# Where the tiles of a gated attention and MLP kernel lie in the SBUF: one stack of pools, or two

## The chip, the cores and the metric

The kernel runs on one core of a Trainium2 chip. The metric is the device time of one execution in microseconds (us), as the median of several runs; smaller is better. A profile comes from one further execution, which has a time of its own. Addresses are bytes from the start of an SBUF partition, in thousands ("51.3 K" is byte 51,328); every tile takes the same bytes in each partition that it uses.

## The reference

`x` is 2048 x 448, float32. A sigmoid gate mixes two branches, row by row:

```
g   = sigmoid(x . gate_w)
q, k, v = x @ wqkv                      # 16 heads of 28
a   = local attention of each row over 8 rows: itself and every second one before it
a   = a @ wo
b   = square(relu(x @ w1 + b1)) @ w2 + b2      # 448 -> 1792 -> 448
out = g * a + (1 - g) * b
```

## The kernel before

**Arithmetic.** Float32 matrices are split into a high part of type float32r and a low part (the remainder), made by ScalarE (copy to float32r) and VectorE (subtract). A product takes three matmuls: high x high, high x low, low x high. Of a matmul's two operands one is loaded into the array (the stationary one; the profile's PEld rows) and the other is streamed through it (the moving one; the PE rows). In a row such as `h<-x1b,w1h` the moving operand stands first, the stationary one second.

**Phase A (to about 110 us).** The 2048 rows are four chunks of 512 columns of the transposed `x`. For each chunk TensorE computes q, k and v. Line 244 does the first 36 matmuls over all 128 rows; after that line 176 (`side_by_side`) issues matmuls of 64 rows in pairs, one for each half of the array. The moving operand is the weight (`wqh`, `wql`, `w7h`, `w7l`), the stationary one `x`. ScalarE evacuates to staging tiles `st` (line 195), and stores go to DRAM (`q_d`, `k_d`, `v_d`). Loads and splits of `w1` and of half of `w2` lie in the same phase.

**Phase B.** The MLP runs over the chunks in the order 3, 0, 1, 2. A step f (14 in each chunk) is a block `h` of 11 matmuls with 512 columns (line 620; moving `x`, stationary `w1`) and a block `b` of 12 matmuls with 448 columns (line 684, `mlp_o`; moving `w2`, stationary `hh` and `hl`), two steps behind. Between them ScalarE does relu and two squares (lines 626 to 628) and VectorE the low part `hl` (line 629). `w2` has two halves: steps 0 to 6 use `w2ah`, `w2al`, steps 7 to 13 `w2bh`, `w2bl`. Beside it GpSimd multiplies and VectorE reduces for the attention (lines 308, 315, 309, 321). From the third chunk on, finished attention tiles are transposed (lines 702, 703; moving `ident`) and multiplied by `wo` (line 725, blocks `a` of 11 matmuls, moving `woh`, `wol`, `wo7`).

**Order.** The program is written in the order that is run: `advance` counts TensorE time, and callbacks (`at`, `soon`, `later`) put splits, loads and attention pieces between. All DMAs are issued by SyncE, in order. `x` of chunks 0 to 2 is spilled to DRAM and reloaded by `x_reload` (line 609) into a ring of five tiles: `x0` to `x3` of `xpool` and a fifth, `x4`, of `phase_b`.

**Where tiles lie.** Pools are stacked one above the other in the order in which they are opened. The pools `phase_a` and `rawp` are closed at line 584 (`actx.close()`), and `phase_b` takes their place; `reuse_waits="tile"` makes each new tile wait for the users of the tiles that lay at its bytes. In the built program this gives:

| tiles | before, K | role for TensorE |
|---|---|---|
| w1h, w1l, w17 | 1.2 to 51.3 | stationary |
| w2ah, w2al | 51.3 to 76.4 | moving |
| ident | 78.3 | moving |
| x of chunks 1 and 3, ring tiles x0 to x3 (`xpool`) | 79.2 to 95.6 | stationary in phase A, moving in B |
| k, v, q of the attention, softmax, products, o | 95.6 to 145.7 | (o: stationary in the transposes) |
| wqh, wql, w7h, w7l (phase A) | 145.7 to 185.4 | moving |
| x of chunks 0 and 2 (phase A) | 185.4 to 201.8 | stationary |
| st, raw (phase A) | 201.8 to 228.9 | |
| w2bh, w2bl (phase B) | 145.7 to 170.8 | moving |
| woh, wol, wo7 (phase B) | 170.8 to 183.4 | moving |
| w2raw, bt (phase B) | 183.4 to 199.5 | |
| ring tile x4 (phase B) | 199.5 to 203.6 | moving |
| hh, hl (phase B) | 203.6 to 215.9 | stationary |
| od, oh, ol, o7, o8 (phase B) | 215.9 to 225.1 | stationary |

Of the kernel before, what the change touches and what calls it, by code (L numbers as in the profile page):

```python
# [8 lines left out]
F32 = mybir.dt.float32  # L9
F32R = mybir.dt.float32r  # L10
# [4 lines left out]
S, D, H, DH, W, F = 2048, 448, 16, 28, 8, 1792  # L15
P = 128
# [3 lines left out]
G = 4  # L20
HG = H // G
C = HG * DH
NF = F // P
CH = 512
NQ = D + 2
# [21 lines left out]
ST_BUFS = 3  # L47
# [4 lines left out]
def gated_mix_kernel(ctx: ExitStack, tc: tile.TileContext, xT, wqkv, w1, w2, wo, b1, b2, out):  # L52
    nc = tc.nc

    def f32(ap):
        return ap.bitcast(F32)
# [6 lines left out]
    x_d = tc.dram_tile([3, 4, P, 2, CH], F32, name="x_d")  # L63
    f_d = tc.dram_tile([2, NS, P, D], F32, name="f_d")

    const = ctx.enter_context(tc.tile_pool(name="const", bufs=1))
    psum = ctx.enter_context(tc.tile_pool(name="psum", bufs=1, space=bass.MemoryType.PSUM))


# [1 line left out]
    w1l = const.tile([P, 3, F], F32R, name="w1l")  # L71
    w17 = const.tile([P, F], F32R, name="w17")
    NFA = NF // 2
    w2ah = const.tile([P, NFA, D], F32R, name="w2ah")
    w2al = const.tile([P, NFA, D], F32R, name="w2al")
    b1t = const.tile([P, NF], F32, name="b1t")
    b2t = const.tile([P, D], F32, name="b2t")
    ident = const.tile([P, P], F32, name="ident")
    mask = const.tile([P, NS, W], F32, name="mask")
    zt = const.tile([P, 2, NS], F32, name="zt")  # L80
    gt = const.tile([P, 2, NS], F32, name="gt")
    g1t = const.tile([P, 2, NS], F32, name="g1t")

    xpool = ctx.enter_context(tc.tile_pool(name="xpool", bufs=1))
    attp = ctx.enter_context(tc.tile_pool(name="attp", bufs=1))
    smp = ctx.enter_context(tc.tile_pool(name="smp", bufs=2))
    prodp = ctx.enter_context(tc.tile_pool(name="prodp", bufs=1))
    opool = ctx.enter_context(tc.tile_pool(name="opool", bufs=1))

    ctx.enter_context(tc.manual_schedule())  # L90
    make_identity(nc, ident)
# [30 lines left out]
    def x_tiles(c, pool):  # L122
        return X([pool.tile([P, 2, CH], F32R, tag=f"x{j}", name=f"x{c}_{j}") for j in range(4)])
# [19 lines left out]


    actx = ExitStack()
    ap = actx.enter_context(tc.tile_pool(name="phase_a", bufs=1, reuse_waits="tile"))
    rawp = actx.enter_context(tc.tile_pool(name="rawp", bufs=2, reuse_waits="tile"))
    wqh = ap.tile([P, 3, 3, NQ], F32R, name="wqh")
    wql = ap.tile([P, 3, 3, NQ], F32R, name="wql")

    w7h = ap.tile([P, 2, NQ], F32R, name="w7h")
    w7l = ap.tile([P, 2, NQ], F32R, name="w7l")

    halo0 = smp.tile([2 * G * HALO, C], F32, tag="lg", name="halo0")
    nc.gpsimd.memset(halo0, 0.0)
# [1 line left out]
    stage = {}  # L157
# [31 lines left out]
    def qkv_evacuate(pt, c, tl, b):  # L189
        par, t = c // 2, (c % 2) * 4 + tl  # L190
        first = (b, t // 2) not in stage
        if first:
            stage[b, t // 2] = ap.tile([P, G, 2, C], F32, tag="stage", name=f"st{c}_{tl}_{b}", bufs=ST_BUFS)
        st = stage[b, t // 2]
        nc.scalar.activation(st[:, :, t % 2], pt[:, :D].rearrange("p (g c) -> p g c", g=G), AF.Copy)  # L195
        if not first:
            stage.pop((b, t // 2))
            t0 = t - t % 2
            dst, off = ((q_d, 0), (k_d, HALO), (v_d, HALO))[b]
            dd = dst[par, :, off:off + SP].rearrange("g (p s) c -> p g s c", s=NS)[:, :, t0:t0 + 2]  # L200
            nc.sync.dma_start(dd.rearrange("p g s c -> p g (s c)"), st.rearrange("p g s c -> p g (s c)"))
        if b == 0:
            nc.scalar.activation(zt[:, par, t:t + 1], pt[:, D:D + 1], AF.Copy)
# [18 lines left out]
    def run(c, todo, steps):  # L222


        a = 0
        for e, done, *turns in steps:
            side_by_side(todo[0][a:e], todo[1][a:e])
            while a < e:
                advance(min(12, e - a) * MM448)
                a = min(a + 12, e)  # L230
            for one, two in turns:
                turn(one, two)
            for b, tl, acc in done:
                assert acc.todo == 0
                qkv_evacuate(acc.pt, c, tl, b)
# [190 lines left out]
    def at(dt, fn):  # L426

        later.append((clock["pe"] + dt, fn))
# [76 lines left out]
        raws.append(raw)  # L505
    raw7 = attp.tile([P, D], F32, tag="q", name="wqraw7")
    nc.sync.dma_start(raw7, wqkv[2, :, 3, :D])
    x = x_tiles(0, ap)
    for k in range(3):
        nc.scalar.activation(wqh[:, k, 0], raws[0][:, k, :NQ], AF.Copy)  # L510
        parts = (slice(0, 256), slice(256, CH)) if k == 0 else (slice(0, CH),)
# [20 lines left out]
    xs = {0: x}  # L532
# [1 line left out]
    SPLIT_AT = {1: 19000.0, 2: 35000.0, 3: 53500.0}  # L534

    def x_begin(c):
        xs[c] = x_tiles(c, xpool if c % 2 else ap)

    def x_more(c):
        xraw[c] = x_load(c)  # L540
# [13 lines left out]
    for c, t in SPLIT_AT.items():  # L554
        when(t, x_begin, c)
        for k in range(4):
            when(t + k * 900.0, lambda c, k: x_split(xraw[c], xs[c], k), c, k)
        if c < 3:
            when(t + 4500.0, x_more, c + 1)
            when(t + 5000.0, lambda c: x_spill(c, xs[c]), c)  # L560
# [8 lines left out]
    for c in range(4):  # L569
        x = xs[c]  # L570
# [13 lines left out]
    actx.close()  # L584


    bp = ctx.enter_context(tc.tile_pool(name="phase_b", bufs=1, reuse_waits="tile"))
    w2bh = bp.tile([P, NFA, D], F32R, name="w2bh")
    w2bl = bp.tile([P, NFA, D], F32R, name="w2bl")
    woh = bp.tile([P, 3, D], F32R, name="woh")  # L590
    wol = bp.tile([P, 3, D], F32R, name="wol")
    wo7 = bp.tile([P, D], F32R, name="wo7")

    def w2hl(f):
        if f < NFA:
# [8 lines left out]
    def x_reload(i, j):  # L604

        c = ORDER[i]
        r = (4 * i + j) % RING
        xt = (xpool if r < 4 else bp).tile([P, 2, CH], F32R, tag=f"x{r}", name=f"x{c}b_{j}")
        nc.sync.dma_start(f32(xt), x_d[c, j])
        return xt  # L610

# [9 lines left out]
        return pt  # L621

    def mlp_act(pt, c, f):
        hh = bp.tile([P, CH], F32R, tag="hh", name=f"hh{c}_{f}", bufs=3)
        hl = bp.tile([P, CH], F32R, tag="hl", name=f"hl{c}_{f}", bufs=3)
        nc.scalar.activation(pt, pt, AF.Relu, bias=b1t[:, f:f + 1])  # L626
        nc.scalar.activation(hh, pt, AF.Square)  # L627
        nc.scalar.activation(pt, pt, AF.Square)  # L628
        at(HL_DELAY, lambda: nc.vector.tensor_sub(hl, pt, f32(hh)))  # L629
        hs[c, f] = (hh, hl)  # L630
# [142 lines left out]
    for i, c in enumerate(ORDER):  # L773
        if i < 3:
            nxt = [x_reload(i + 1, j) for j in range(early)]
        for f in range(NF):
            pt = mlp_h(x, c, f)
            if f == NF - 4:
                for tl in range(4):
                    fin_fetch(c // 2, (c % 2) * 4 + tl)  # L780
            if f == NF - 1 and i < 3:
                nxt += [x_reload(i + 1, j) for j in range(early, 4)]
            advance(11 * MM512)
            mlp_act(pt, c, f)
            pend.append((c, f))
            lag = 0 if f == NF - 1 and i < 3 else 2
            wo_ready()
            if i > 0:
                wo_step()
            while len(pend) > lag:  # L790
                mlp_o(*pend.pop(0))
                advance(12 * MM448)
        if i < 3:
            x = X(nxt)
# [52 lines left out]
```

## Time and profile before

| | us |
|---|---|
| median of 3 runs (436.4 to 436.87) | 436.61 |
| the profiled execution | 436.64 |
| its span, first to last instruction | 434.9 |
| around the span | 1.7 |
| TensorE busy in the span (2516 matmuls) | 429.1 |
| weight loads busy (2516) | 385.9 |
| GpSimd, VectorE, ScalarE busy | 274.8, 257.9, 179.3 |
| granted TensorE clock, mean | 0.998 |

How to read it: matmuls follow one another through the array, so the duration of one (363 ns for 448 columns) is longer than the distance to the next (about 200 ns); a busy TensorE row is no measure of speed. What counts is how far apart the starts of successive blocks are. The chain of waits in order of time shows that: each piece has its start, its length and the number of matmuls in it.

### The profile page before, as it was taken

The numbers are of one execution on the slowest core, as the hardware profiler recorded it, in microseconds if no ns is written. First come the engines' busy times: TensorE is split into PE (matmuls) and PEld (weight loads), VectorE is DVE, ScalarE is ACT, GpSimd is POOL, SyncE is SP. The second block draws the span as 40 slices with busy tenths as digits, with TensorE's granted clock in tenths as the row PEclk, the third lists the DMA queues.
The fourth block names the chain that finished last, engine by engine and source line by source line (L and its number), as shares of the span: only waits on it lengthen the run. The fifth ranks groups of instructions, "written<-read, shape, count | busy, mean of one in ns | idle before, by whom it ended". The sixth has DMA issues, their size and how long they took to land.

```text
span 434.9 us, 6554 instructions
## 1 busy us (share of the span) xinstructions
PE 429.1 (99%) x2516; PEld 385.9 (89%) x2516; DVE 257.9 (59%) x384; ACT 179.3 (41%) x372; POOL 274.8 (63%) x167
## 2 busy tenths in 40 slices
PE   8999999999999999999999999999999999999996
PEld 7999999999888888888888888888888888888895
DVE  4421322375589977976646776644676856755453
ACT  3542454444554444533433454333523433334530
POOL 1000001940999999999998897945499998785000
PEclk9999999999999999999999999999999999999999
DMA  7989899938723307703203651401427400210013
GB/s 224 365 299 346 223 391 287 356 80 298 260 89 119 142 2 259 254 29 121 78 2 121 223 199 36 151 21 44 142 86 260 172 1 0 76 68 0 2 63 128
DMA packets 33199, 65.44 MB, mean 150 GB/s; under 512 B 2704, under 2 KB 26256, under 8 KB 32784
## 3 DMA queue, kind: packets, MB, share of 16 engines
q1 hardware_dynamic: 33168, 65.02, 43.0%
q8 instruction: 20, 0.33, 0.3%
q14 instruction: 11, 0.09, 0.1%
HBM read 41.23 MB, written 23.77 MB: 149 GB/s over the span
## 4 chain that ended last, share of the span: by engine, by line
PE 97%; DMA 1%; DVE 1%; SPq 0%; issue 0%; ACT 0%
PE h L620 33%; PE b L684 31%; PE qkv L176 22%; PE a L725 8%; PE oT L702 1%; PE qkv L244 1%; DMA xraw<-xT 1%; PE oT L703 0%; SPq L499 0%; SPq L494 0%; DVE bt L660 0%; DVE wql L513 0%; DVE x L514 0%; DVE ol L102 0%; ACT o L101 0%
## 5 line engine op out<-in xcount | busy, mean ns | idle before, releaser
L308 POOL TENSOR_TENSOR qk<-q,k 128x896 f32<-128x896 f32 x64 | 138.6, 2193 | 103.4 <-DMA k<-k_d 72.5
L315 POOL TENSOR_TENSOR av<-lg,v 128x896 f32<-128x896 f32 x64 | 122.3, 2006 | 13.2 <-DVE o L321 7.1
L626 ACT ACTIVATE h<-h,b1t 128x512 f32<-128x512 f32 x56 | 37.0, 662 | 157.6 <-PE h L620 157.6
L176 PE MATMUL qkv<-wqh,x 64*128 64x448 f32 (+1 forms) x528 | 86.8, 363 | 0.0
L629 DVE TENSOR_TENSOR hl<-h,hh 128x512 fp32r<-128x512 f32 x56 | 38.6, 688 | 62.1 <-ACT h L628 61.9
L309 DVE TENSOR_REDUCE lg<-qk 128x32 f32<-128x896 f32 x64 | 66.9, 1076 | 3.9 <-POOL qk L308 3.9
L321 DVE TENSOR_REDUCE o<-av 128x112 f32<-128x896 f32 x64 | 66.6, 1072 | 0.0
L176 PEld LDWEIGHTS qkv<-wqh,x 64*128 64x128 f32 x528 | 59.6, 185 | 0.6
L176 PE MATMUL qkv<-wql,x 64*128 64x448 f32 (+1 forms) x264 | 56.5, 363 | 0.0
L195 ACT ACTIVATE st<-qkv 128x448 f32<-128x448 f32 x48 | 24.7, 544 | 48.4 <-PE qkv L176 39.9
L684 PE MATMUL b<-w2bl,hh 128*128 128x448 f32 x112 | 40.9, 365 | 0.0
L684 PE MATMUL b<-w2bh,hl 128*128 128x448 f32 x112 | 40.9, 365 | 0.0
L684 PE MATMUL b<-w2bh,hh 128*128 128x448 f32 x112 | 40.9, 365 | 0.0
L684 PE MATMUL b<-w2ah,hh 128*128 128x448 f32 x112 | 40.7, 364 | 0.0
L684 PE MATMUL b<-w2ah,hl 128*128 128x448 f32 x112 | 40.6, 362 | 0.0
L684 PE MATMUL b<-w2al,hh 128*128 128x448 f32 x112 | 40.5, 362 | 0.0
L627 ACT ACTIVATE hh<-h 128x512 fp32r<-128x512 f32 x56 | 33.6, 599 | 3.6 <-DMA v_d<-st 1.9
L628 ACT ACTIVATE h<-h 128x512 f32<-128x512 f32 x56 | 33.2, 593 | 0.0
L176 PEld LDWEIGHTS qkv<-wql,x 64*128 64x128 f32 x264 | 30.8, 185 | 0.3
L620 PE MATMUL h<-x1b,w1h 128*128 128x512 f32 x84 | 28.6, 395 | 0.0
L620 PE MATMUL h<-x2b,w1h 128*128 128x512 f32 x84 | 28.5, 393 | 0.0
L620 PE MATMUL h<-x0b,w1h 128*128 128x512 f32 x84 | 28.4, 391 | 0.0
(108 smaller groups left out, 761.0 us busy)
## 6 DMA issues: line engine op xcount, KB each, us to landing
k<-k_d SPq DMA_DIRECT2D x8, 840.0 KB, 5.1
v<-v_d SPq DMA_DIRECT2D x8, 840.0 KB, 4.6
x_d<-x SPq DMA_DIRECT2D x12, 512.0 KB, 5.5
q_d<-st SPq DMA_DIRECT2D x8, 448.0 KB, 8.0
k_d<-st SPq DMA_DIRECT2D x8, 448.0 KB, 5.1
v_d<-st SPq DMA_DIRECT2D x8, 448.0 KB, 6.7
w1raw<-w SPq DMA_DIRECT2D x4, 896.0 KB, 9.9
q<-q_d SPq DMA_DIRECT2D x8, 448.0 KB, 3.4
```

The lines of the kernel that those rows point to most:

```text
L176: nc.tensor.matmul(acc.pt[:, :acc.n], a[rows], w[rows], start=acc.todo == 21, stop=acc.todo == 1)
L308: nc.gpsimd.tensor_mul(pr, q[:, s:s + 1].to_broadcast([P, W, C]), k[:, s:s + W])
L309: pending.append(lambda: nc.vector.tensor_reduce(lg[:, s], pr.rearrange("p w (h d) -> p w h d", h=HG), axis=AX.X, op=ALU.add))
L315: nc.gpsimd.tensor_mul(pr.rearrange("p (h d) w -> p w h d", h=HG), lg[:, s][:, :, :, None].to_broadcast([P, W, HG, DH]), v[:, s:s + W].rea ...
L321: pending.append(lambda: nc.vector.tensor_reduce(o[:, g * C:(g + 1) * C], pr, axis=AX.X, op=ALU.add))
L620: nc.tensor.matmul(pt, w, a, start=i == 0, stop=i == len(pr) - 1)
L626: nc.scalar.activation(pt, pt, AF.Relu, bias=b1t[:, f:f + 1])
L627: nc.scalar.activation(hh, pt, AF.Square)
L628: nc.scalar.activation(pt, pt, AF.Square)
L629: at(HL_DELAY, lambda: nc.vector.tensor_sub(hl, pt, f32(hh)))
L684: nc.tensor.matmul(bps[tl][:, :D], a[:, sl], w, start=f == 0 and i == 0, stop=f == NF - 1 and i == 2)
L725: nc.tensor.matmul(pa[:, :D], a, w, start=i == 0, stop=i == len(pr) - 1)
```

## The change

All pools get a side: `side="left"` pools stack up from the lower end, `side="right"` pools from the upper end. Tiles that TensorE streams go to left pools (`low`, `xpool`, `wqp`, then `phase_b_low`), everything else to right pools. `phase_a` is cut into `wqp` (left), `xap` and `stp` (right), and `hh`, `hl` get a pool of their own, `hidden`. No shape, buffer count or instruction is changed.

| tiles | after, K |
|---|---|
| w2ah, w2al | 1.2 to 26.2 |
| ident | 26.2 |
| x of chunks 1 and 3, ring tiles x0 to x3 | 26.8 to 43.1 |
| wqh, wql, w7h, w7l (phase A) | 43.1 to 82.8 |
| w2bh, w2bl; woh, wol, wo7; ring tile x4 (phase B) | 43.1 to 68.2; 68.2 to 80.8; 80.8 to 84.9 |
| st; raw; x of chunks 0 and 2 (phase A) | 83.2 to 94.0; 94.0 to 110.4; 110.4 to 126.8 |
| w2raw, bt; od to o8; hh, hl (phase B) | 89.1 to 105.2; 105.2 to 114.5; 114.5 to 126.8 |
| o, products, softmax, k, v, q | 126.8 to 176.9 |
| w1h, w1l, w17 | 176.9 to 227.0 |

```diff
-    const = ctx.enter_context(tc.tile_pool(name="const", bufs=1))
+    low = ctx.enter_context(tc.tile_pool(name="low", bufs=1, side="left"))
+    const = ctx.enter_context(tc.tile_pool(name="const", bufs=1, side="right"))
...
-    w2ah = const.tile([P, NFA, D], F32R, name="w2ah")
-    w2al = const.tile([P, NFA, D], F32R, name="w2al")
+    w2ah = low.tile([P, NFA, D], F32R, name="w2ah")
+    w2al = low.tile([P, NFA, D], F32R, name="w2al")
...
-    ident = const.tile([P, P], F32, name="ident")
+    ident = low.tile([P, P], F32, name="ident")
...
-    xpool = ctx.enter_context(tc.tile_pool(name="xpool", bufs=1))
-    attp = ctx.enter_context(tc.tile_pool(name="attp", bufs=1))
+    xpool = ctx.enter_context(tc.tile_pool(name="xpool", bufs=1, side="left"))
+    attp = ctx.enter_context(tc.tile_pool(name="attp", bufs=1, side="right"))
...
-    ap = actx.enter_context(tc.tile_pool(name="phase_a", bufs=1, reuse_waits="tile"))
-    rawp = actx.enter_context(tc.tile_pool(name="rawp", bufs=2, reuse_waits="tile"))
-    wqh = ap.tile([P, 3, 3, NQ], F32R, name="wqh")
+    wqp = actx.enter_context(tc.tile_pool(name="wqp", bufs=1, side="left", reuse_waits="tile"))
+    xap = actx.enter_context(tc.tile_pool(name="xap", bufs=1, side="right", reuse_waits="tile"))
+    rawp = actx.enter_context(tc.tile_pool(name="rawp", bufs=2, side="right", reuse_waits="tile"))
+    stp = actx.enter_context(tc.tile_pool(name="stp", bufs=ST_BUFS, side="right", reuse_waits="tile"))
+    wqh = wqp.tile([P, 3, 3, NQ], F32R, name="wqh")
...
-    bp = ctx.enter_context(tc.tile_pool(name="phase_b", bufs=1, reuse_waits="tile"))
-    w2bh = bp.tile([P, NFA, D], F32R, name="w2bh")
-    woh = bp.tile([P, 3, D], F32R, name="woh")
+    bl = ctx.enter_context(tc.tile_pool(name="phase_b_low", bufs=1, side="left", reuse_waits="tile"))
+    hp = ctx.enter_context(tc.tile_pool(name="hidden", bufs=3, side="right", reuse_waits="tile"))
+    bp = ctx.enter_context(tc.tile_pool(name="phase_b", bufs=1, side="right", reuse_waits="tile"))
+    w2bh = bl.tile([P, NFA, D], F32R, name="w2bh")
+    woh = bl.tile([P, 3, D], F32R, name="woh")
...
-        xt = (xpool if r < 4 else bp).tile([P, 2, CH], F32R, tag=f"x{r}", name=f"x{c}b_{j}")
+        xt = (xpool if r < 4 else bl).tile([P, 2, CH], F32R, tag=f"x{r}", name=f"x{c}b_{j}")
...
-        hh = bp.tile([P, CH], F32R, tag="hh", name=f"hh{c}_{f}", bufs=3)
-        hl = bp.tile([P, CH], F32R, tag="hl", name=f"hl{c}_{f}", bufs=3)
+        hh = hp.tile([P, CH], F32R, tag="hh", name=f"hh{c}_{f}")
+        hl = hp.tile([P, CH], F32R, tag="hl", name=f"hl{c}_{f}")
```

## The prediction

> **What bounds the kernel now.** I read the page first, then who waited for whom on TensorE, then the chain of waits in order of time.
>
> ```profile
> PE 429.1 (99%) x2516; PEld 385.9 (89%) x2516; DVE 257.9 (59%) x384; ACT 179.3 (41%) x372; POOL 274.8 (63%) x167
> ...
> PE 97%; DMA 1%; DVE 1%; SPq 0%; issue 0%; ACT 0%
> ```
>
> TensorE is busy all along, and 97% of the chain that ends last is TensorE. Its list of waits has a single entry:
>
> ```profile
> PE warm L487 <- DVE zero L485: 1.2, 1, 1.2
> ```
>
> So nothing that another engine does can shorten this kernel. Only a smaller distance between the starts of matmuls can. The chain in order of time (start, length, matmuls) shows that equal blocks have unequal lengths. First the MLP of chunk 3 (left column: start in us):
>
> ```profile
> 141.84 2.40 PE b L684 x12
> 144.24 2.49 PE h L620 x11
> 146.73 2.40 PE b L684 x12
> 149.13 2.49 PE h L620 x11
> 151.62 2.43 PE b L684 x12
> 154.06 2.52 PE h L620 x11
> ```
>
> then chunk 2 near the end, then chunk 1 with its `wo` blocks, then all of phase A's pairs:
>
> ```profile
> 376.31 2.40 PE b L684 x12
> 378.71 2.54 PE h L620 x11
> 381.25 2.45 PE b L684 x12
> 383.69 2.54 PE h L620 x11
> ```
>
> ```profile
> 271.11 2.57 PE h L620 x11
> 273.68 0.33 PE oT L702 x3
> 274.00 0.11 PE oT L703
> 274.11 2.23 PE a L725 x11
> ```
>
> ```profile
> 13.81 95.86 PE qkv L176 x928
> ```
>
> The reader is to see three things. A `b` block takes 2.40 us (200.0 ns for each matmul of 448 columns) while it streams `w2a` (51 to 76 K), and 2.43 to 2.45 from the step on which it streams `w2b` (146 to 171 K): at 151.62 in chunk 3, at 381.25 in chunk 2, with nothing else different. An `h` block takes 2.49 (226.7 each) in chunk 3, whose four `x` tiles lie at 79 to 96 K, and 2.53, 2.57 and 2.54 in chunks 0, 1 and 2, one of whose tiles is `x4` at 199 K. And 200.0 and 226.7 differ by 26.7 ns for 64 columns, 0.417 ns a column: 448 and 512 columns are 186.7 and 213.3, and both leave the same 13.3 ns, a floor on which every stretch with only low moving tiles sits. The spread does not follow what else runs: attention occupies GpSimd in 141 to 149 us too.
>
> Is it the moving or the stationary operand? `w2a` sits on the floor with `hh`, `hl` at 204 to 216 K, and chunk 3's `x` with `w1` at 1 to 51 K, so a stationary operand may be high or low. Its load is as long from either end (ns min/median/max in the list of line 684, then 620):
>
> ```profile
> L684 PEld LDWEIGHTS b<-w2ah,hh x112: 187/188/190, 117.0 to 377.8; 128*128 128x128 f32 x112
> ```
>
> ```profile
> L620 PEld LDWEIGHTS h<-x,w1h x84: 186/188/188, 109.6 to 170.4; 128*128 128x128 f32 x84
> ```
>
> So I take the height of the moving tile as the cause. One thing is less plain: `x4` is 2 or 3 of the 11 matmuls in a block, and an excess of 0.07 us would make these 25 ns longer, more than any is; the low tiles behind a high one are slower too, for a few matmuls. Whether it is a slope, or a step between 96 K and 146 K, the trace cannot say; the change takes every moving tile to 1 to 85 K, and either gives the floor.
>
> **The change part by part.** The five engines' programs of both kernels agree row by row; only addresses differ, and the waits of nine rows around the change of phase.
>
> *h blocks.* Floor 2.493 (the step from 119.77 to 149.13 us repeats six times, 4.893 each, less 2.400 for `b`). Excess: chunk 3, five blocks that follow `w2b`, 0.03 each, 0.15; chunk 0, 14 x 0.04, 0.55; chunk 1, 14 x 0.07, 1.0; chunk 2, 14 x 0.045, 0.6. Sum **2.3 us**. If the lateness behind `x4` comes from the jump between tiles (104 to 120 K apart now, 38 to 58 K after), up to half of the 2.15 in chunks 0 to 2 stays: 1.2 is the lower end. I take 2.3, since `x` to `w2a` is a jump of 3 to 44 K now and leaves nothing.
>
> *b blocks with w2b.* Seven steps in each of four chunks, 28 blocks of 2.43 to 2.45 against 2.40: 28 x 0.037 = **1.05 us**.
>
> *a blocks.* 16 of 2.23 against 11 x 0.200 = 2.20: 0.48. Each stands behind a transpose, whose hand-over may hold part of it; bounds 0.2 and 0.48, I take **0.4**.
>
> *Pairs of phase A.* 936 matmuls are 468 pairs; 95.86 us are 204.8 ns a pair, where 448 columns at the floor are 200.0 and the mean of 448 and 450 columns 200.3. The moving weights lie at 146 to 185 K. No pair is seen with low weights, so this is the unknown. At most all of it goes: 468 x 4.5 = 2.1 us, less about 0.2 of visible stops. At least nothing, if pairs hinder each other wherever their weights lie; the nearest row, `w2b` at the same height, has 2.9 ns, 468 x 2.9 = 1.35. I take **1.6**, between that row and all of it, since a pair reads two streams; both ends stay in the range.
>
> *Below 51 K* no moving tile lies now. 51 to 76 K and 79 to 96 K have the same 13.3 ns, so I expect neither gain nor loss from going lower: 0.
>
> *Other engines.* Their tiles move up (attention operands from 96-146 K to 127-177 K, `w1` to 177-227 K). TensorE waits for none of them; 0, with the attention case below as the price.
>
> *Waits at 111 us.* Before, `hh` of step 0 lay on a staging tile, and ScalarE waited 1.9 us for the last store (`v_d<-st`, landed at 114.85). That wait goes and gives nothing, as TensorE was busy with `h` blocks meanwhile. In its place the first `w2raw` load lies on staging tiles, so SyncE holds it from 111.33 to about 114.9, and behind it the reload of `x0b` and three more `w2raw` loads. It lands 4.7 us after its issue (111.33 to 116.00 now), at 119.6. ScalarE's copy `w2ah<-w2raw` moves from 117.66 to 119.7, and relu, squares and `hl` of step 2 behind it are done at about 122.8. TensorE wants them for its third `b` block at 127.16: 4.3 us to spare. Cost 0; were the cover gone, each us of lateness would be one on the path.
>
> Sum: 2.3 + 1.05 + 0.4 + 1.6 = 5.35 us. The profiled execution took 436.64 (span 434.9 and 1.7 around it), 0.03 from the median: 436.64 - 5.35 = **431.3 us**. With the ends of the unknowns (h 1.2 to 2.4, a 0.2 to 0.48, pairs 0 to 2.1) the gain is 2.45 to 6.0: 430.6 to 434.2.
>
> **The rivals.**
>
> *Attention sets the end.* The last transposes at 403.64 wait for the last reduction, done at 400.8. TensorE will be there 4.9 us earlier. If attention does not move with it, the tail starts 2.1 us earlier instead of 4.9, and with the tail's own 0.3 the time is 436.64 - 2.4 = 434.2. For it: GpSimd runs the last eight products without a pause. Against: before 366 us GpSimd is held by VectorE, whose reductions stand behind `hl` of TensorE's steps (10.9 us idle before 310.5, 0.7 to 1.2 at 355, 360 and 365), so attention is paced by TensorE and moves with it; and after its last product at 397.1 the reduction waits behind one more `hl`.
>
> *Height does not matter.* The blocks differ by which tile they read, and I infer height. Then the change does not do what it moves tiles for: 436.6. For it: no tile is seen at two heights in one role. Against: three kinds of moving tile (`w2`, `x`, `wo`) at five places all fit. The Trainium skill speaks for this rival: "SBUF — State Buffer", section "SBUF: two separate sides", says that TensorE never waits on anyone at the SBUF and lets only the port pair shared by VectorE and GpSimd contend; it knows no dependence on the address. The trace disagrees at least in this, that 448 columns take 200.0 ns from one tile and 203 from another.
>
> *Weights from the top (slower).* `w1`, stationary in all 616 matmuls of line 620, goes from 1-51 K to 177-227 K. If a load from there delays the next stream, the time is 431.3 + 0.616 x the ns each. It decides from 8.6 ns each (436.6). Were the 13.3 ns between streams doubled, it would be 431.3 + 8.2 = 439.5. Against: the loads of `hh` at 204 to 216 K last the same 188 ns and sit on the floor. For: there they stand 200 ns apart, and none lies over 216 K but `oh` to `o8`, whose blocks are above the floor.
>
> **How the numbers follow.** Forecast 0.81 (430.2 to 434.2, with 0.4 below 430.6 for the 10 ns to which the chain's pieces are given); attention 0.07 (434.2); no effect of height 0.06 (436.6); slower 0.06 (439.5). Predicted 431.3. Range 430.2 to 434.2: the first case with the ends of its unknowns, which reaches the second. Faster by over 0.2% (0.9 us, about what a measurement of this kernel can tell from no change) holds in the first two: 0.88; within 0.2%: 0.06; slower: 0.06.
>
> **What would show it.** In the profile after, the chain should have every `b` block at 2.40, every `h` block at 2.49, `a` blocks near 2.20, and the pairs of phase A in some 94.3 us instead of 95.9. The copy of the first `w2raw` should start two us later against `h` of step 2, with no wait of TensorE. It would be wrong if `h` blocks of chunk 3 rise above 2.49 (weights from the top), if `w2b` blocks stay at 2.44 (no height), or if TensorE idles before the last transposes (attention).

## The result, and the profile after

| | before, us | after, us |
|---|---|---|
| median of 4 runs each (lowest to highest) | 436.66 (436.4 to 436.87) | 441.2 (441.04 to 441.35) |
| span of the profiled execution | 434.9 | 439.2 |
| mean granted TensorE clock | 0.998 | 0.999 |

The ratio after to before is 1.0104, 95% interval 1.0087 to 1.0122. The kernel became 1% slower; 431.3 had been predicted. The number falls outside the range and its sign is wrong.

The page of the kernel after: TensorE is again busy all along, and the chain that ends last is again TensorE.

```profile
PE 433.4 (99%) x2516; PEld 385.8 (88%) x2516; DVE 266.6 (61%) x384; ACT 179.4 (41%) x372; POOL 276.8 (63%) x167
...
PE 97%; DMA 1%; DVE 1%; SPq 0%; issue 0%; ACT 0%
```

TensorE's waits after, the same single entry at its new line number:

```profile
PE warm L491 <- DVE zero L489: 1.2, 1, 1.2
```

So the 4.3 us of span are again in the distances between matmuls. Lines have moved: `h` is L626, `b` L690, `a` L731, the pairs L180. The chain in order of time (start, length, matmuls), first the stretches of chunk 3, then chunk 2, then chunk 1 with `wo`, then phase A:

```profile
142.31 2.46 PE b L690 x12
144.77 2.57 PE h L626 x11
147.33 2.46 PE b L690 x12
149.79 2.57 PE h L626 x11
152.36 2.46 PE b L690 x12
154.82 2.57 PE h L626 x11
```

```profile
375.10 2.46 PE b L690 x12
377.56 2.56 PE h L626 x11
380.12 2.46 PE b L690 x12
382.58 2.57 PE h L626 x11
```

```profile
268.80 0.11 PE oT L709
268.90 2.26 PE a L731 x11
271.16 2.46 PE b L690 x12
```

```profile
13.39 95.86 PE qkv L180 x925
```

The reader is to see that the difference between tiles is gone, as predicted, but upwards: every `b` block takes 2.46 us, with either half of `w2`, and every `h` block 2.57, with or without `x4`. None is on the floor (2.40 and 2.49). The pairs take the same 95.86 us. By starts of single matmuls (mean block of a kind and chunk, after minus before, times the number of blocks) the terms are: `h` +2.0 us, `b` with `w2a` +1.6, `b` with `w2b` +0.7, `a` +0.4; and the first `h` block starts 0.4 us earlier, from a shorter start-up. The sum is +4.3, the difference of the spans.

### The profile page after: what moved, and what is told of

Its sections match the earlier page's. It is cut to its first block, busy times and chain, and to the rows that moved or that the text cites. A ratio compares the mean times of both kernels' runs of the same rounds, so it can differ in the third digit from the quotient of the medians.

```text
span 439.2 us, 6552 instructions
## 1 busy us (share of the span) xinstructions
PE 433.4 (99%) x2516; PEld 385.8 (88%) x2516; DVE 266.6 (61%) x384; ACT 179.4 (41%) x372; POOL 276.8 (63%) x167
## 4 chain that ended last, share of the span: by engine, by line
PE 97%; DMA 1%; DVE 1%; SPq 0%; issue 0%; ACT 0%
PE h L626 33%; PE b L690 31%; PE qkv L180 22%; PE a L731 8%; PE oT L708 1%; PE qkv L248 1%; DMA xraw<-xT 1%; PE oT L709 0%; SPq L503 0%; SPq L498 0%; DVE bt L666 0%; DVE wql L517 0%; DVE x L518 0%; DVE ol L104 0%; ACT o L103 0%
## 5 line engine op out<-in xcount | busy, mean ns | idle before, releaser
L319 POOL TENSOR_TENSOR av<-lg,v 128x896 f32<-128x896 f32 x64 | 125.1, 2055 | 13.6 <-DVE o L325 7.1
L180 PE MATMUL qkv<-wqh,x 64*128 64x448 f32 (+1 forms) x528 | 87.4, 363 | 0.0
L180 PEld LDWEIGHTS qkv<-wqh,x 64*128 64x128 f32 x528 | 60.4, 185 | 0.5
L180 PE MATMUL qkv<-wql,x 64*128 64x448 f32 (+1 forms) x264 | 57.3, 363 | 0.0
L690 PE MATMUL b<-w2ah,hh 128*128 128x448 f32 x112 | 41.3, 369 | 0.0
L690 PE MATMUL b<-w2bh,hh 128*128 128x448 f32 x112 | 41.2, 368 | 0.0
L690 PE MATMUL b<-w2ah,hl 128*128 128x448 f32 x112 | 41.1, 367 | 0.0
L690 PE MATMUL b<-w2bh,hl 128*128 128x448 f32 x112 | 41.1, 367 | 0.0
L690 PE MATMUL b<-w2bl,hh 128*128 128x448 f32 x112 | 41.1, 367 | 0.0
L690 PE MATMUL b<-w2al,hh 128*128 128x448 f32 x112 | 41.0, 366 | 0.0
L180 PEld LDWEIGHTS qkv<-wql,x 64*128 64x128 f32 x264 | 31.5, 185 | 0.3
L626 PE MATMUL h<-x,w1h 128*128 128x512 f32 x84 | 28.8, 396 | 0.0
L626 PE MATMUL h<-x2b,w1h 128*128 128x512 f32 x84 | 28.7, 395 | 0.0
L626 PE MATMUL h<-x0b,w1h 128*128 128x512 f32 x84 | 28.7, 395 | 0.0
```

Of the source, the lines that this page charges most:

```text
L180: nc.tensor.matmul(acc.pt[:, :acc.n], a[rows], w[rows], start=acc.todo == 21, stop=acc.todo == 1)
L319: nc.gpsimd.tensor_mul(pr.rearrange("p (h d) w -> p w h d", h=HG), lg[:, s][:, :, :, None].to_broadcast([P, W, HG, DH]), v[:, s:s + W].rea ...
L626: nc.tensor.matmul(pt, w, a, start=i == 0, stop=i == len(pr) - 1)
L690: nc.tensor.matmul(bps[tl][:, :D], a[:, sl], w, start=f == 0 and i == 0, stop=f == NF - 1 and i == 2)
```

## The theories

Tiles that had sat on the floor fell off it although they moved down (`w2a` from 51 to 1 K, chunk 3's `x` from 79 to 27 K). Three theories:

- **A, each operand's own alignment.** The right-hand stack ends at byte 229,344 and holds tiles of odd sizes, so `hh`, `hl` and `w1` now start 32 and 224 bytes above a multiple of 256; before they started at 64 and 128. Among moving tiles before, those on the floor started at 128, `w2b`, `wo` and `x4` at 64.
- **B, the part of the SBUF.** Weights high up, or both operands of a matmul too far apart or in wrong parts, delay the stream (the rival "weights from the top").
- **C, formed after the first experiments: the distance of the two operands.** What counts is (start of the stationary operand − start of the moving one) modulo 256 bytes; neither height nor an operand's own alignment matters. Below, this is the distance, and the residue of an address is what is left of it modulo 256.

Which slice of a tile is read makes no difference to these residues: a row of `w2` is 1792 bytes, one of `w1` 7168, a slice of 128 columns 512, all multiples of 256. The rows of the q, k and v weights are 1800 bytes, so these spread over many residues.

## The experiments

The versions named a_ start from the kernel after, those named b_ and m_ from the kernel before. Padding tiles, which nothing reads or writes, shift all that is stacked behind them. The kernel before, run beside them, took 436.28 us (median) beside the first eight and 436.42 beside a_pairs and the m_ kernels. No padding changes an instruction.

**a_pad96: the kernel after with 96 bytes more at the top.** Every right-hand tile below moves by 96 bytes; its height stays.

```diff
+    const.tile([P, 24], F32, name="pad")      # after, behind g1t
```

> The changed kernel with 96 unused bytes at the end of the pool const, so that everything on the upper side lies 96 bytes lower: w1 starts on a multiple of 128 bytes instead of 96 beyond one, hh, hl, oh, ol 64 beyond one instead of 32. Theory A (alignment: a moving operand off a multiple of 128 bytes, or a stationary one off a multiple of 64, costs some ns a matmul; height costs nothing): all h blocks 2.49 us, all b blocks 2.40, a blocks 2.20 to 2.23, phase A's pairs as before; time 436.6 - 2.3 - 1.05 - 0.4 = 432.9 us. Theory B (the part of the SBUF: w1 near the top and hh in the middle are slow to load): blocks stay at 2.57 and 2.46, time 441.2.

Measured: 434.97 us (two of the ten runs took 438.3), ratio of the means to before 0.9983 (0.9962 to 1.0004). Against the kernel after, 96 bytes are worth some 6 us. B falls: height is as in the kernel after. In its chain of chunk 0 `h` is on the floor, but `b` is not:

```profile
205.78 2.43 PE b L691 x12
208.21 2.49 PE h L627 x11
210.70 2.43 PE b L691 x12
```

A had `b` at 2.40 and 432.9. Half of A failed: `hh` at residue 192, a multiple of 64 as A asks, is not undisturbed.

**b_pad64: the kernel before with 64 bytes ahead of the attention's products,** so that `w2b`, `wo`, `x4`, `hh` and `hl` start at 128 instead of 64.

```diff
+    padp = ctx.enter_context(tc.tile_pool(name="padp", bufs=1))
+    padp.tile([P, 16], F32, name="pad")       # before, ahead of prodp
```

> The kernel before with 64 unused bytes ahead of prodp, so that everything above (o, phase_a, phase_b) lies 64 bytes higher: w2b, wo and x4 start on a multiple of 128 bytes instead of 64 beyond one. Theory A (alignment): all h blocks 2.49 us, all b blocks 2.40, a 2.20 to 2.23; time 432.9 us. Theory B (part of the SBUF): 64 bytes are nothing, blocks as before (h 2.49 to 2.57, b 2.40 and 2.44), time 436.6.

Measured: 435.97, ratio 0.9994 (0.9984 to 1.0003). The chain of chunk 3:

```profile
144.26 2.51 PE h L622 x11
146.76 2.43 PE b L686 x12
149.20 2.51 PE h L622 x11
151.71 2.43 PE b L686 x12
```

`x4` now has the residue of the other `x` tiles, and the `h` blocks are nearly equal in all chunks (means 2.506 to 2.511). But `b` with `w2a` rose from 2.40 to 2.43, although `w2a` did not move. What moved is `hh`, to the residue of `w2a`. `w2b` stays at 2.43: moved along with `hh`, it too has the residue of its partner, as before. A cannot say this.

**b_w1_32 and b_w2_off: 32 bytes ahead of w1 (96 behind it), and 32 and 96 around each half of w2.** One run each.

> The kernel before with 32 unused bytes ahead of w1h and 96 after w17: w1 alone starts 32 bytes beyond a multiple of 128, all other tiles keep their place within 128 bytes. Theory A (alignment): the h blocks of chunk 3 go from 2.49 to 2.54 to 2.57 us, those of the other chunks to about 2.57, b blocks with w2a of chunk 3 stay at 2.40; time about 436.6 + 1.1 + 0.5 + 0.4 = 438.6 us. Theory B (part of the SBUF): w1 stays at the bottom, no block changes, 436.6.

> The kernel before with pads of 32 and 96 bytes around w2a and around w2b: w2a starts 32 beyond a multiple of 128 instead of on one, w2b 96 beyond instead of 64; all other tiles keep their place within 128 bytes. Theory A (alignment): b blocks with w2a go from 2.40 to 2.43 to 2.46 us, those with w2b stay at 2.43 to 2.46, h blocks of chunk 3 rise by the 0.03 that they have behind w2b now; time about 436.6 + 1.1 + 0.4 = 438.1 us. If only multiples of 32 mattered: unchanged. Theory B (part of the SBUF): unchanged, 436.6.

Measured: 438.95 and 440.02. B (436.6) falls again. The first has `h` at 2.56 to 2.57 in every chunk and `b` with `w2a` nearly unchanged; it fits A in size. The second misses A by 1.9 us: `b` rose to 2.46 as meant, but `h` rose too, to 2.56, without a pad at `w1` or between the `x` tiles. The pads around `w2a` had moved `x` by 128 bytes against `w1`. That was not meant, and it led to theory C.

**b_all32: all tiles of the kernel before moved by the same 32 bytes.** A and C differ most here.

```diff
+    const.tile([P, 8], F32, name="pad0")      # before, ahead of w1h
```

> The kernel before with 32 unused bytes ahead of w1h: every tile lies 32 bytes higher, all distances between tiles are as before. Theory A (alignment of each operand by itself): every start is off a 64-byte boundary, so h blocks 2.55 or more, b blocks 2.46, time about 441. Theory C (only the distance between the moving and the stationary operand counts, taken modulo 256 bytes): every block as in the kernel before (h 2.50, 2.53, 2.56, 2.54 in chunks 3, 0, 1, 2; b 2.40 with w2a, 2.43 with w2b), time 436.3.

Measured: 436.28, ratio 1.0005 (0.9996 to 1.0014). Every tile has moved off its multiple of 64 by 32 bytes, as far as `hh` is off one in the kernel after, and every block is as long as in the kernel before:

```profile
148.63 2.49 PE h L621 x11
151.12 2.43 PE b L685 x12
153.56 2.52 PE h L621 x11
```

A falls. Only a relation between tiles is left.

**b_w1_192: 192 bytes ahead of w1, 64 behind it,** which changes the distance of `w1` to the `x` tiles and nothing else.

> The kernel before with 192 unused bytes ahead of w1h and 64 after w17: w1 starts on a multiple of 64 bytes as before, but 192 beyond a multiple of 256 when counted from x (before: 0); every other distance is as before modulo 256. Theory A (alignment, a stationary operand needs 64): nothing changes, 436.3. Theory C (distance modulo 256; seen so far for 512 columns: 0 gives the floor, 64 to 160 and 224 give 5.6 to 7.1 ns more): h blocks 2.55 to 2.57 in all chunks, time about 436.3 + 56 x 0.03 = 438.0.

Measured: 436.52 in one run. The size that C gave (438.0) was missed. The place was right: chunk 3's `h` blocks rose from a mean of 2.502 to 2.526 (without the first, at the change of phase). In the other chunks `x4` got distance 0 while `x0` to `x3` lost it, and these two cancel nearly (2.531, 2.560, 2.537 to 2.533, 2.553, 2.543). The excess of 512 columns at the distance 192 is (2.526 − 2.493) / 11 = 3.0 ns, half of what the other wrong distances have.

**a_best and b_best: the good distances, from both kernels.** a_best is a_pad96 with 128 bytes more ahead of the attention's pool, so that `hh` has the distance 192 to all of `w2` and `w1` 0 to all of `x`. b_best gives the kernel before the same distances and leaves every tile at its old height.

```diff
+    padp = ctx.enter_context(tc.tile_pool(name="padp", bufs=1, side="right"))
+    padp.tile([P, 32], F32, name="pad2")      # a_best: a_pad96, ahead of attp
```

```diff
+    bp.tile([P, 16], F32, name="pad0")        # b_best: before, ahead of w2bh
...
+            bp.tile([P, 48], F32, name="pad1")   # behind x4
```

> The changed kernel (two stacks) with 96 unused bytes in const and 128 in a pool of their own ahead of attp: w1 lies 0 from x, hh and hl 192 from w2, oh and ol 192 from wo, each modulo 256. Theory C (distance): all h blocks 2.49, all b blocks 2.40, time 435.0 - 56 x 0.03 - 16 x 0.03 = 432.8. Theory A (alignment): as the run with the 96 bytes alone, 435.0. Theory B (part of the SBUF) fell with the runs before.

> The kernel before (one stack) with 64 unused bytes ahead of w2bh and 192 after x4: w2b, wo and x4 come to the same place modulo 256 as w2a and the other x tiles have, hh, hl, oh, ol stay. Distances as in the two-stack kernel with 96 and 128 bytes, heights as before. Theory C (distance): all h blocks 2.49, all b blocks 2.40, time 436.3 - 2.2 - 1.05 - 0.4 = 432.7, the same as that kernel. If height counted beside it, the two would differ.

Measured: 432.87, ratio 0.9924 (0.9912 to 0.9937), and 433.09, ratio 0.9932 (0.9918 to 0.9945). The chain of chunk 3 in a_best, then in b_best:

```profile
143.77 2.49 PE h L629 x11
146.26 2.40 PE b L693 x12
148.67 2.49 PE h L629 x11
```

```profile
146.39 2.40 PE b L687 x12
148.79 2.49 PE h L623 x11
151.28 2.40 PE b L687 x12
153.68 2.49 PE h L623 x11
```

In one `w1` lies at 177 to 227 K, `w2b` at 43 K and `x4` at 81 K; in the other `w1` at 1 K, `w2b` at 146 K and `x4` at 199 K. All blocks are on the same floor (means over all chunks but 1: `b` 2.401, `h` 2.493, in both). Height counts for nothing that these runs can see. Both beat both kernels.

**m_32_128, m_224_96, m_w1_32: the other distances,** each b_best with pads around `w2a`, `w2b` or `w1`.

> The one-stack kernel with the right distances, where w2a is moved so that hh and hl are 32 from it, and w2b so that they are 128 from it (modulo 256; the right distance is 192). Theory C: both leave the floor, b blocks 2.43 to 2.47 us with either half, h blocks 2.49 to 2.52; time about 433.1 + 56 x 0.04 = 435.3. If only distances that are no multiple of 64 cost more than 3 ns a matmul: w2a 2.46, w2b 2.43.

> The same with distances 224 (w2a) and 96 (w2b). Theory C: both leave the floor, 2.43 to 2.47; 96 was 4.4 ns a matmul (2.45) in a kernel where other blocks were off too; time about 435.3.

> The one-stack kernel with the right distances, where w1 alone is moved by 32 bytes, so that it is 32 from x instead of 0. Theory C: h blocks leave the floor, 2.55 to 2.57 us as at 64 to 160, b blocks at 2.40 to 2.42; time about 433.1 + 56 x 0.07 = 437.0. If it is the multiple of 64 that counts for 512 columns, the same; if 32 is near enough to 0, 2.50 and 433.5.

Measured: 437.01, 435.77 and 437.05. The third was expected within 0.1 us. The other two came 1.7 and 0.5 us above. Their `b` blocks cost about what was expected, 2.6 and 2.5 us in all over b_best, against 2.2 (single blocks 2.445 at 32, 2.451 at 128, 2.472 at 224, 2.418 at 96). The rest is in the `h` blocks, whose distance is 0 as before: 1.2 us more in m_32_128 (2.52 against 2.49), 0.3 in m_224_96. The expectation had named that length and had not put it into the time. The idea that distances off a multiple of 64 alone cost much falls: 32 and 128 cost nearly the same. In m_224_96 chunk 0 shows `w2a` at the distance 224, beside `h` blocks near the floor:

```profile
206.06 2.47 PE b L690 x12
208.53 2.49 PE h L626 x11
211.02 2.47 PE b L690 x12
```

**a_pairs: a_best with the q, k and v weights at one residue.** Their rows are laid out so that each starts at 128 modulo 256; then `x` of chunks 0 and 2 is at the distance 192 and that of chunks 1 and 3 at 0.

> The two-stack kernel with both pads (96 and 128 bytes), and in phase A each row of wqh, wql, w7h, w7l laid on the same place modulo 256 (rows of 1800 bytes spread over tiles of 512 columns for q and 448 for k and v, so that all start 128 beyond a multiple of 256; the v part of w7 lies in the pool of o). x of chunks 0 and 2 is then 192 from every streamed row, x of chunks 1 and 3 is 0 from it. Theory C, if pairs of 64 rows follow the same distances as whole matmuls: chunks 0 and 2 at 200.3 ns a pair instead of 204.8 (216 pairs, -1.0 us), chunks 1 and 3 at 203.0 (252 pairs, -0.4 us): time 432.9 - 1.4 = 431.5. If two streams in the array hinder each other whatever their addresses: 432.9.

Measured: 433.07, ratio 0.9923 (0.9909 to 0.9936): no gain over a_best, 1.6 us above the expectation. A pair takes 202 ns in chunks 0 and 2, against 205; 204 and 207 in chunks 1 and 3, against 204 and 205 (without the last two pairs, where phase A ends, chunk 3 has 205 against 204). So the distance acts in phase A too, but this layout of the weights serves two chunks and brings the others nothing: the whole stretch takes 95.37 us against 95.79 in a_best, a gain of 0.4 where 1.4 was expected. All of that was lost again, 0.1 us in a later start and 0.6 at a new wait in chunk 0. TensorE's list of waits in a_pairs:

```profile
PE warm L502 <- DVE zero L500: 1.2, 1, 1.2
PE qkv L259 <- DVE x L527: 0.8, 1, 0.8
PE b L701 <- DVE hl L646: 0.3, 1, 0.3
```

The wait for `hl`, 0.3 us in that list and 0.6 by the starts of the matmuls, is at 185 us, where the chain that ends last comes over GpSimd's products and VectorE's splits of `wo`, which stand ahead of `hl`. One of 0.4 us is in a_pad96 too. These two are the runs whose `h` blocks begin earliest (108.8 and 108.9 us, the others at 109.1 or later). That fits TensorE having nearly caught up with the attention there; then more gain in phase A would be given back at 185 us, which no run has tried.

## Why the prediction was wrong, by its own steps

- **"So I take the height of the moving tile as the cause": the step that failed.** The rows that it rested on were read rightly: fast blocks with `w2a` and chunk 3's `x`, slow ones with `w2b`, `x4` and `wo`. Its "with nothing else different" was not so: in that one layout height and distance went together. The distance of `hh` to `w2a` was 192 and to `w2b` 0, that of `w1` to `x0` to `x3` 0 and to `x4` 64. What I held for the step between 96 K and 146 K was the residue of the tiles that happened to lie above it. Pads of 96 and 128 bytes in the kernel after, which lower no tile by more than 224 bytes, brought some 8 us (441.2 to 432.87, beside 436.66 and 436.28 for the kernel before).
- **"Is it the moving or the stationary operand?" was the wrong question.** I excluded the stationary one because it was seen high and low on the floor, and because its load lasts 188 ns from either end. It does so after, too, in the slowest blocks:

```profile
L626 PEld LDWEIGHTS h<-x,w1h x84: 186/188/192, 109.2 to 171.4; 128*128 128x128 f32 x84
```

  The length of the load does not show the disturbance; that of the matmul does. In the list of line 620, then 626, the median matmul of `x` with `w1l` goes from 389 to 398 ns:

```profile
L620 PE MATMUL h<-x,w1l x42: 389/389/398, 109.9 to 170.4; 128*128 128x512 f32 x42
```

```profile
L626 PE MATMUL h<-x,w1l x42: 391/398/400, 109.5 to 171.4; 128*128 128x512 f32 x42
```

- **The size of the terms was nearly right, for another cause.** In a_best, which has what I thought the change would bring, the single matmuls give: `h` −2.1 us (2.3 predicted), `b` with `w2b` −0.95 (1.05), `a` −0.3 (0.4). The floor of 13.3 ns, 2.40 and 2.49 hold in a_best to the last digit. In the kernel after the same terms are +2.0, +0.7 and +0.4, and "below 51 K", taken as 0, became +1.6, since `w2a` lost its distance of 192.
- **Pairs of phase A, 1.6 us: 0.** The 95.86 us did not move in the kernel after, nor by over 0.1 us in a_best and b_best. I took them as disturbed by height, with `w2b` as the nearest row. With rows 1800 bytes apart their distances are spread in all these layouts, and 95.8 to 95.9 us would be an average over them; a_pairs gives 202 ns where nearly all distances are 192.
- **"One thing is less plain" was the hint.** An excess of 25 ns on `x4` was "longer than any is", and the low tiles behind it were slow too. A disturbed matmul leaves the next ones late: in the kernel before, `h` blocks of chunk 3, all at distance 0, take 2.49 behind `w2a` and 2.52 behind `w2b`. A view that did not fit the height was in the text, and I made a bound of it (1.2 to 2.4 for `h`) instead of a rival.
- **Rivals.** "Weights from the top" had the sign and nearly the time (431.3 + 0.616 x 16 ns would be 441.2), and the prediction named its mark, `h` blocks of chunk 3 above 2.49. As a mechanism it falls: in a_best the weights lie up there and `h` is at 2.493. "Height does not matter" is what proved true, but its time, 436.6, supposed that nothing else changes with the addresses. The two were given 0.06 each.
- **Waits at 111 us: cost 0, right.** ScalarE no longer waits for `v_d<-st`. SyncE did hold the first `w2raw` load, to 114.18 us; ScalarE copied from it at 116.72, not at 119.7, since the load took 2.5 us and not 4.7. TensorE did not notice.
- **Attention: right that it moves with TensorE.** The last transposes start at 407.71 after a `b` block, 4.1 us later than before. a_best, 3.4 us faster than the kernel before, has no wait of TensorE for it; the waits for `hl` in a_pad96 and a_pairs are at another place and 0.3 to 0.4 us long.
- **The Trainium skill.** By the Trainium skill, "SBUF — State Buffer", section "Who interferes with whom", TensorE waits on no one at the SBUF. No run here shows it waiting for another engine there. But its pace depends on how the starts of its own two operands lie to each other, which that sentence does not cover: 441.2 against 432.87 us with the same instructions.

## What to carry to other kernels

In a dense stream of matmuls with a weight load each (float32r and 128 x 128 weights here; other types were not tried), look at the two operands' start addresses as a pair, modulo 256 bytes, before anything else about where a tile lies: two pads, of 96 and 128 bytes, were worth 1.8% here (1.0104 against 0.9924 of the kernel before). One layout cannot tell two properties of an address apart, however many rows agree; a cause read off a single layout should get a rival for each other property that varies with it. And a change that moves all tiles moves all such properties at once, so its risk is on both sides even if no instruction changes.

## What the runs showed of the hardware

The length of a block by the distance (stationary − moving) modulo 256 bytes, from starts of single matmuls. A `b` entry is the mean of a chunk's blocks with one half of `w2`, all of them at this distance; the floor is 2.400. The first `h` block of chunk 3 is left out.

| distance, bytes | 12 matmuls of 448 columns, us | from | 11 matmuls of 512 columns, us | from |
|---|---|---|---|---|
| 0 | 2.432 | b_pad64 | 2.493 | a_best, b_best |
| 32 | 2.445 | m_32_128 | 2.564 | m_w1_32 |
| 64 | 2.428 | a_pad96 | not alone in a block | |
| 96 | 2.418 | m_224_96 | 2.569 | after |
| 128 | 2.451 | m_32_128 | 2.557 | b_w2_off, chunk 3 |
| 160 | 2.460 | after | 2.570 | b_w1_32, chunk 3 |
| 192 | 2.401 | a_best, b_best | 2.526 | b_w1_192, chunk 3 |
| 224 | 2.472 | m_224_96 | not alone in a block | |

The worst is 6.0 ns more for each matmul of 448 columns and 7.0 for one of 512: 3%. The `b` and `h` blocks stand between one another, and a disturbed one leaves the next few matmuls late, so part of what a distance costs can stand in the neighbour's length: the `h` blocks of m_32_128, at distance 0, took 2.52, and distance 96 gave 2.410 to 2.475 in b_w2_off, where the `h` blocks were disturbed too. The period is not 32, 64 or 128, as 0 and 128 differ, and it is not 512: `w1` starts 0 modulo 512 from the tiles of `xpool` in a_best and 256 from them in b_best, and the `h` blocks of both are on the floor. "TensorE: Matmul & The Clock Gate" in the Trainium skill, section "Step-by-step: what each phase is for", says that loading the next tile's weights takes no read bandwidth from the running matmul. The table shows that the length of the same matmuls depends on where the weights start against the stream, so the two reads are not without effect on each other if that load is the partner, which no run isolates.

Open is why 448 columns are best at 192 and 512 at 0. 448 and 512 columns are 1792 and 2048 bytes, both multiples of 256, so the length of a stream shifts no residue; which bytes the two reads have reached when they meet was not measured. Nor was it tried whether the partner that matters is the matmul's own weights or the load for the next one, which runs meanwhile (in the kernel before the first load of line 684 starts at 117.0 us, its matmul at 117.2): within a block both have the same residue. A layout with `x` of all four chunks at 192 to the q, k and v weights was not tried either.
